# Gates of chunks 1 to 5 computed on 80 partitions, one for each chunk and head, with transfers issued from ScalarE's queue

## The chip, the core and the metric

The kernel runs on one core of one Trainium2 chip. Five engines work beside each other, each through a queue of its own in order: TensorE (PE in the profile, with its weight loads as PEld), VectorE (DVE), ScalarE (ACT), GpSimd (Pool) and SyncE (SP), which here only issues DMAs. The metric is the time of one execution on the device in microseconds; lower is better.

## What is computed

An mLSTM layer over 2 x 8 heads with 768 tokens of 40 channels, then two feed-forward layers on its 1536 tokens of 320 channels. What matters here is the first part, and in it the gates:

```python
for t in range(S):
    m_new = np.maximum(f_gate[:, :, t] + m, i_gate[:, :, t])
    f_stab = np.exp(f_gate[:, :, t] + m - m_new)
    i_stab = np.exp(i_gate[:, :, t] - m_new)
    m = m_new
    C = f_stab * C + i_stab * einsum("bhd,bhe->bhde", vt, kt)
    n = f_stab * n + i_stab * kt
    y[:, :, t] = sigmoid(o_gate) * (C @ qt) / max(|n . qt|, 1)
x = relu_like(y @ w_in) @ w_out              # 320 -> 2048 -> 320
out = sum_e P[:, e] * (relu(x @ w1[e]) @ w2[e])  # 8 experts, 320 -> 1024 -> 320, P by 8 rounds of scaling
```

All products are made in halves of a split (high and low parts in the float32r type), and the result is float32.

## The kernel before

**Tiles and stages.** The 768 tokens are cut into six chunks of 128; a tile is one chunk of one batch entry with its 8 heads, so there are 12 tiles, numbered chunk by chunk. Within a chunk the recurrence becomes matrix products: a scan along the columns makes the 128 x 128 decay matrix of each head (L383, four heads at a time), it is multiplied with the scores (L385), and TensorE multiplies the result with the weighted values (L400). What comes from earlier chunks is the state `Cst` (L395, L407, L412, L440). The result is transposed (L446) and split into `XH` and `XL` (L114, L116).

Four stages of the first feed-forward layer (`STAGES`, `gemm_k` at L124, L541 to L547, `moe1_g2` at L557 to L561) are woven into the tiles; then come the eight experts, which take most of the time (L124 and L704 to L706). The weights of the first layer come as 64-bit floats and are decoded by VectorE and ScalarE (L212 to L256).

**Gates.** Of the gates, two copies of the 16 rows (one for each batch entry and head) lie on 32 partitions, 768 columns each: `g_i`, `g_f` and the running maximum `g_m`, in the tile `g_all`. `gate_exps(a, b)` makes the maximum of columns a to b by a scan (L307), then on the forget gates L310 and L311 and an Exp (L312), on the input gates L313 and an Exp (L314). `gate_prods` makes the running products of the forget gates within each chunk (L326), and writes the forget gates of chunks 1 to 5 to a DRAM buffer `g_d` (L333); `load_g` reads them back for each tile, broadcast to 128 partitions, as the tile `G0` or `G1` (L145). `gate_by_token` transposes gates and products, so that tokens lie on partitions (L340, L341, copied at L342 into `gt`), and `gate_ends` makes the products at the chunks' ends (L346, L353, L354, into `lend`). Chunk 0 has its own short way: its decay comes from products with a one-hot matrix (L376), not from DRAM. The code calls:

```python
gate_exps(0, L); gate_prods(0, 1); gate_by_token(0, 1); gate_exps(L, S)
starts = [attn(0, ("at", "ax")), attn(1, ("g2", "g2"))]
step = 0
while len(done) < 2:
    for g in starts:
        next(g, None)
        warm(WD)
    step += 1
    if step == GP:
        gates_rest()        # gate_prods(1, NCH), gate_by_token(1, NCH), gate_ends(), load_g
    if step in PUMP:
        pump_w()            # one more piece of decoded weights
```

**Order.** The code is written tile by tile; a framework then lists the instructions of each engine in an order of its own by estimated times, keeps the dependencies with semaphores, and each engine works through its list in order. `warm` adds products of a zero tile (L296) of a fixed number. SP issues the DMAs in its list's order; each DMA adds to one of eight semaphores, which are taken in turn, and one that takes a semaphore again waits until the DMA that had it before has landed.

Of the kernel before, what the change touches and what calls it, by code (L numbers as in the profile page):

```python
# [36 lines left out]
GP = 8  # L37
# [11 lines left out]
def mlstm_moe_moe_kernel(  # L49
# [76 lines left out]
    with ExitStack() as atx:  # L126
# [172 lines left out]
        gp.memset(ones, 1.0)  # L299
# [16 lines left out]
        def gate_prods(c0, c1):

            if c0 == 0:
                act(out=g_s, in_=g_f[:, 0:L], func=ACTF.Copy)
                vec.scalar_tensor_tensor(  # L320
                    out=g_s, in0=f(g_s), scalar=cst[0:32, C_N16 : C_N16 + 1], in1=g_f[:, 0:L], op0=ALU.mult, op1=ALU.add,
                )
                vec.tensor_copy(g_s[:, 0:1], zer[:, 0:1])
            for c in range(c0, c1):
                cs = slice(c * L, (c + 1) * L)
                vec.tensor_tensor_scan(out=g_m[:, cs], data0=g_f[:, cs], data1=zer, initial=1.0, op0=ALU.mult, op1=ALU.add)  # L326
            if c0:
                gp.tensor_copy(
                    g_f[:, c0 * L : c1 * L].rearrange("p (c t) -> p c t", t=L)[:, :, 0:1], zer[:, 0 : c1 - c0].unsqueeze(2)
                )  # L330
                for j in range(4):
                    o = j // 2 * 8 + j % 2
                    nc.sync.dma_start(g_d[j * 4 : j * 4 + 4, :], g_f[o : o + 7 : 2, L:S])  # L333

        def gate_by_token(c0, c1):
            p = bank("g1")
            for c in range(c0, c1):
                cs = slice(c * L, (c + 1) * L)
                o = (c - c0) * 32
                nc.tensor.transpose(p[:, o : o + 16], g_i[0:16, cs], ident[0:16, 0:16])  # L340
                nc.tensor.transpose(p[:, o + 16 : o + 32], g_m[0:16, cs], ident[0:16, 0:16])  # L341
# [462 lines left out]
```

## Time and profile before

| | |
|---|---|
| time, median of 3 runs (lowest, highest) | 995.71 us (994.46, 996.32) |
| the profiled execution, its own time | 994.85 us |
| its span, first to last instruction | 993.1 us |
| TensorE busy | 979.6 us, 99% of the span |
| VectorE busy | 470.1 us, 47% |
| ScalarE busy | 344.8 us, 35% |
| GpSimd busy | 31.2 us, 3% |

The span is the time between the first and the last instruction of the profiled execution; its own time has the start and the end around it. Shares are means over stages of different kinds: VectorE has nearly all its work of the first 140 us without a pause, and little later. A row of a timeline says when an instruction, or a row of equal ones, started, how long it was busy, and behind brackets how long its engine had been idle before and what released it.

### The profile page before, as it was taken

The numbers are of one execution on the slowest core, as the hardware profiler recorded it, in microseconds if no ns is written. First come the engines' busy times: TensorE is split into PE (matmuls) and PEld (weight loads), VectorE is DVE, ScalarE is ACT, GpSimd is POOL, SyncE is SP. The second block draws the span as 40 slices with busy tenths as digits, with TensorE's granted clock in tenths as the row PEclk, the third lists the DMA queues.
The fourth block names the chain that finished last, engine by engine and source line by source line (L and its number), as shares of the span: only waits on it lengthen the run. The fifth ranks groups of instructions, "written<-read, shape, count | busy, mean of one in ns | idle before, by whom it ended". The sixth has DMA issues, their size and how long they took to land.

```text
span 993.1 us, 13483 instructions
## 1 busy us (share of the span) xinstructions
PE 979.6 (99%) x5520; PEld 861.8 (87%) x5520; DVE 470.1 (47%) x853; ACT 344.8 (35%) x622; POOL 31.2 (3%) x43
## 2 busy tenths in 40 slices
PE   9999899999999999999999999999999999999998
PEld 5789788887878899999999999989999999999997
DVE  9999977655563644322522432242253234222222
ACT  3743684477773224211411321141132123111111
POOL 2212101000000000000000000000000000000000
PEclk9999999999999999999999999999999999999999
DMA  5865413000132002100400210030021002000000
GB/s 171 263 169 172 143 57 99 12 1 0 47 113 75 1 1 64 54 1 1 117 1 1 74 44 1 7 111 1 1 87 31 1 17 72 1 1 1 27 27 27
DMA packets 42190, 51.91 MB, mean 52 GB/s; under 512 B 3360, under 2 KB 35744, under 8 KB 42128
## 3 DMA queue, kind: packets, MB, share of 16 engines
q1 hardware_dynamic: 42128, 51.05, 17.3%
q8 instruction: 43, 0.70, 0.3%
q14 instruction: 19, 0.16, 0.0%
HBM read 49.03 MB, written 2.01 MB: 51 GB/s over the span
## 4 chain that ended last, share of the span: by engine, by line
PE 89%; DVE 5%; ACT 3%; DMA 1%; issue 1%; SPq 0%; DVEq 0%; ACTq 0%
PE bk_g L124 41%; PE bk_g L704 9%; PE bk_g L706 8%; PE bk_g L705 8%; PE bk_ax L705 3%; PE bk_ax L704 3%; PE bk_ax L706 3%; PE bk_at L400 2%; PE bk_g L296 2%; PE bk_g L559 2%; PE bk_g L558 1%; PE bk_g L557 1%; PE bk_at L379 1%; DMA raw<-in_w_dram 1%; PE bk_g L561 1%
## 5 line engine op out<-in xcount | busy, mean ns | idle before, releaser
L124 PE MATMUL bk_g<-XH,wk 128*128 128x512 f32 (+1 forms) x1240 | 399.8, 388 | 1.6 <-DVE gs L545 1.6
L724 DVE SCALAR_TENSOR_TENSOR lo<-bk_g,hi 128x512 fp32r<-128x512 f32 x192 | 132.6, 691 | 372.6 <-ACT hi L723 371.7
L124 PE MATMUL bk_g<-XL,wk 128*128 128x512 f32 (+1 forms) x744 | 285.4, 384 | 0.0
L723 ACT ACTIVATE hi<-bk_g 128x512 fp32r<-128x512 f32 x192 | 114.9, 599 | 453.2 <-PE bk_g L124 453.0
L124 PEld LDWEIGHTS bk_g<-XH,wk 128*128 128x128 f32 x1240 | 230.6, 188 | 45.1 <-DVE gs L545 2.6
L704 PE MATMUL bk_g<-wf,hi 128*128 128x320 f32 x576 | 177.4, 308 | 1.1 <-ACT hi L723 1.1
L705 PE MATMUL bk_g<-wf,hi 128*128 128x320 f32 x576 | 177.0, 307 | 0.0
L706 PE MATMUL bk_g<-wf,lo 128*128 128x320 f32 x576 | 176.9, 308 | 0.0
L124 PEld LDWEIGHTS bk_g<-XL,wk 128*128 128x128 f32 x744 | 140.0, 188 | 21.4
L704 PEld LDWEIGHTS bk_g<-wf,hi 128*128 128x128 f32 x576 | 108.0, 187 | 8.1 <-ACT hi L723 1.6
L705 PEld LDWEIGHTS bk_g<-wf,hi 128*128 128x128 f32 x576 | 108.1, 188 | 6.3
L706 PEld LDWEIGHTS bk_g<-wf,lo 128*128 128x128 f32 x576 | 107.9, 187 | 0.0
L705 PE MATMUL bk_ax<-wf,hi 128*128 128x320 f32 x192 | 59.1, 308 | 0.0
L704 PE MATMUL bk_ax<-wf,hi 128*128 128x320 f32 x192 | 59.0, 307 | 0.0
L706 PE MATMUL bk_ax<-wf,lo 128*128 128x320 f32 x192 | 58.4, 304 | 0.0
L545 DVE TENSOR_TENSOR gs<-bk_g,gs 128x512 f32<-128x512 f32 x40 | 27.5, 688 | 26.8 <-ACT gs L543 26.4
L541 ACT ACTIVATE gs<-bk_g 128x512 f32<-128x512 f32 x48 | 28.5, 594 | 28.7 <-PE bk_g L124 28.1
L738 DVE SCALAR_TENSOR_TENSOR acc<-bk_g,P,acc 128x320 f32<-128x320 f32 x63 | 30.8, 545 | 15.3 <-PE bk_g L706 15.3
L531 DVE TENSOR_TENSOR wf<-raw,wf 128x640 fp32r<-128x640 f32 x32 | 26.3, 826 | 20.7 <-ACT wf L530 20.5
L704 PEld LDWEIGHTS bk_ax<-wf,hi 128*128 128x128 f32 x192 | 36.1, 188 | 0.0
L706 PEld LDWEIGHTS bk_ax<-wf,lo 128*128 128x128 f32 x192 | 36.1, 188 | 0.0
L705 PEld LDWEIGHTS bk_ax<-wf,hi 128*128 128x128 f32 x192 | 35.9, 187 | 0.0
(198 smaller groups left out, 999.6 us busy)
## 6 DMA issues: line engine op xcount, KB each, us to landing
raw<-in_w_dram SPq DMA_DIRECT2D x32, 320.0 KB
raw<-in_w_dram SPq DMA_DIRECT2D x32, 256.0 KB
kvo_t<-in_kvo_dram SPq DMA_DIRECT2D x12, 484.0 KB
raw<-in_w_out_dram SPq DMA_DIRECT2D x8, 640.0 KB
raw<-in_w_in_dram SPq DMA_DIRECT2D x8, 512.0 KB
raw<-in_w_dram SPq DMA_DIRECT2D x64, 64.0 KB
qk<-in_qk_dram SPq DMA_DIRECT2D x24, 160.0 KB
G<-g_d SPq DMA_DIRECT2D x5, 512.0 KB
```

What stands on the lines that cost most here:

```text
L124: return [mm(dst, a, b, start=i == 0, stop=i == len(seq) - 1) for i, (a, b) in enumerate(seq)]
L296: mm(to, wz, wz[:, 0:1].to_broadcast([128, 512]), start=True, stop=True)
L400: mm(pa[:, h * 41 : (h + 1) * 41], A[h % 2][:, h // 2, :], vw[:, h, :], start=True, stop=True)
L531: vec.tensor_tensor(out=wf[:, fs, 320:640], in0=rs[n], in1=f(wf[:, fs, 0:320]), op=ALU.subtract)
L541: act(out=t, in_=pg, func=ACTF.Relu, scale=-1.0, bias=1.0)
L545: dve_at.append(vec.tensor_tensor(out=g, in0=pg, in1=t, op=ALU.max))
L704: mm(pp[i], hi[:, ts], wf[:, ff, 0:320], start=st, stop=False)
L705: mm(pp[i], hi[:, ts], wf[:, ff, 320:640], start=False, stop=False)
L706: mm(pp[i], lo[:, ts], wf[:, ff, 0:320], start=False, stop=sp)
L723: act(out=hi, in_=pg, func=ACTF.Relu)
L724: vec.scalar_tensor_tensor(out=lo, in0=pg, scalar=0.0, in1=f(hi), op0=ALU.max, op1=ALU.subtract)
L738: vec.scalar_tensor_tensor(out=acc[:, t, :], in0=pp[i], scalar=P[:, t, e : e + 1], in1=acc[:, t, :], op0=ALU.mult, op1=ALU.add)
```

## The change

The gates of chunk 0 are made first (`gates_first`), with their product in a tile of its own, `g_p`. Of chunks 1 to 5 only the scan for the maximum still runs on 640 columns. Then fifteen small transfers, three for each chunk, bring the raw gates (L338 of the new code, from DRAM) and the maximum (L339, from `g_m`) onto 80 partitions, 16 for each chunk, with 128 columns each (`gl_f`, `gl_i`, `gl_m`). All later steps run on these: three element-wise ones and two Exp (L314 to L318), one product scan instead of five (L343), one write of `g_d` with 80 rows (L345), two transposes instead of ten (L347, L348), z and the product for `lend` (L355, L358). The fifteen transfers and the write of `g_d` are issued by ScalarE. The later gates are asked for after step 2 instead of step 8 (`GP`). `load_g` reads each tile's gates in two DMAs of four heads instead of one of eight. The tile `ones` is made at the start of the experts' part instead of at the kernel's start. Ten of the fifteen transfers read from DRAM what SP has also loaded; those of chunks 1 and 2 land where `g_f` lies, so they wait for the long scan.

```diff
@@ load_g
             c, b = divmod(t, 2)
-            nc.sync.dma_start(
-                G1 if t % 2 else G0, g_d[b * 8 : b * 8 + 8, (c - 1) * L : c * L].unsqueeze(0).to_broadcast([128, 8, L])
-            )
+            g, r = G1 if t % 2 else G0, (c - 1) * 16 + b * 8
+            for hf in range(2):
+                nc.sync.dma_start(
+                    g[:, hf * 4 : hf * 4 + 4, :], g_d[r + hf : r + 7 + hf : 2, :].unsqueeze(0).to_broadcast([128, 4, L])
+                )
@@ gates
-GP = 8
+GP = 2
-        gate_exps(0, L)
-        gate_prods(0, 1)
-        gate_by_token(0, 1)
-        gate_exps(L, S)
+        gates_first()
+        def gate_exps(fg, ig, m, m_new):
+            vec.tensor_tensor(out=fg, in0=fg, in1=m, op=ALU.add)
+            vec.tensor_tensor(out=fg, in0=fg, in1=m_new, op=ALU.subtract)
+            act(out=fg, in_=fg, func=ACTF.Exp)
+            vec.tensor_tensor(out=ig, in0=ig, in1=m_new, op=ALU.subtract)
+            act(out=ig, in_=ig, func=ACTF.Exp)
+
+        def gates_first():
+
+            gate_max(0, L)
+            gate_exps(g_f[:, 0:L], g_i[:, 0:L], g_m[:, 0:L], g_m[:, 1 : L + 1])
...
+            gate_max(L, S)
+
+            for c in range(1, NCH):
+                for x, o in ((gl_f, S), (gl_i, 0)):
+                    nc.scalar.dma_start(x[(c - 1) * 16 : c * 16], gates[0:16, o + c * L : o + (c + 1) * L])
+                nc.scalar.dma_start(gl_m[(c - 1) * 16 : c * 16], g_m[0:16, c * L : (c + 1) * L + 1])
+
+        def gates_later():
+            gate_exps(gl_f, gl_i, gl_m[:, 0:L], gl_m[:, 1 : L + 1])
+            vec.tensor_tensor_scan(out=gl_p, data0=gl_f, data1=cst[0:NLR, C_Z : C_Z + 1].to_broadcast([NLR, L]), initial=1.0, op0=ALU.mult, op1=ALU.add)
+            gp.tensor_copy(gl_f[:, 0:1], cst[0:NLR, C_Z : C_Z + 1])
+            nc.scalar.dma_start(g_d, gl_f)
+            p = bank("g1")
+            nc.tensor.transpose(p[:, 0:NLR], gl_i, ident[0:NLR, 0:NLR])
+            nc.tensor.transpose(p[:, NLR : 2 * NLR], gl_p, ident[0:NLR, 0:NLR])
...
@@ experts
+        ones = m2.tile([128, 128], F32, name="ones")
+        gp.memset(ones, 1.0)
```

What it does to the lists is seen at three places. In the rows, names are those of the tiles, with buffer numbers; in brackets stand the semaphores that an instruction waits for: those of an engine's progress (`DVE_49`, `PE_49`, `Activation_49`, `Pool_49`) and the eight of the DMAs (`DMAHW0_49` to `DMAHW7_49`). Line numbers of the changed kernel are higher by 3 to 5 for the same code.

VectorE, from the long scan of the maximum on, before:

```order
L307 SCALAR_TENSOR_TENSOR g_all_80<-g_all_80 32x640
L310 TENSOR_TENSOR g_all_80<-g_all_80 32x640 [waits DVE_49]
L326 SCALAR_TENSOR_TENSOR g_all_80<-g_all_80,cst_64 32x128 [waits DMAHW2_49,Activation_49]
L320 SCALAR_TENSOR_TENSOR g_s_110<-g_s_110,cst_64,g_all_80 32x128 [waits Activation_49]
L311 TENSOR_TENSOR g_all_80<-g_all_80 32x640 [waits DVE_49]
L323 CAST g_s_110<-cst_64 32x1 [waits DVE_49]
L313 TENSOR_TENSOR g_all_80<-g_all_80 32x640
L326 SCALAR_TENSOR_TENSOR g_all_80<-g_all_80,cst_64 32x128 [waits DVE_49,Activation_49]
L326 SCALAR_TENSOR_TENSOR g_all_80<-g_all_80,cst_64 32x128 x2
L383 SCALAR_TENSOR_TENSOR G0_90<-bk_at_166,id4_116 128x512 [waits PE_49,Pool_49]
L326 SCALAR_TENSOR_TENSOR g_all_80<-g_all_80,cst_64 32x128
L385 TENSOR_TENSOR A_207<-bk_at_171,G0_90 128x512 [waits DVE_49,PE_49]
```

The same place in the changed kernel:

```order
L309 SCALAR_TENSOR_TENSOR g_all_79<-g_all_79 32x640
L329 SCALAR_TENSOR_TENSOR g_p_111<-g_all_79,cst_64 16x128 [waits DMAHW7_49,Activation_49]
L325 SCALAR_TENSOR_TENSOR g_s_110<-g_s_110,cst_64,g_all_79 32x128 [waits Activation_49]
L328 CAST g_s_110<-cst_64 32x1 [waits DVE_49]
L388 SCALAR_TENSOR_TENSOR G0_90<-bk_at_176,id4_117 128x512 [waits PE_49,Pool_49]
L390 TENSOR_TENSOR A_234<-bk_at_181,G0_90 128x512 [waits DVE_49,PE_49]
L388 SCALAR_TENSOR_TENSOR scr_87<-bk_g2_190,id4_117 128x512 [waits PE_49]
L314 TENSOR_TENSOR g_all_79<-g_all_79,gl_m_86 80x128 [waits DMAHW5_49,DMAHW6_49,DMAHW4_49,DMAHW7_49,DMAHW3_49,DMAHW0_49]
L317 TENSOR_TENSOR g_all_79<-g_all_79,gl_m_86 80x128 [waits DMAHW2_49,DMAHW1_49]
L315 TENSOR_TENSOR g_all_79<-g_all_79,gl_m_86 80x128 [waits DVE_49]
L390 TENSOR_TENSOR scr_87<-bk_g2_195,scr_87 128x512 [waits PE_49]
L388 SCALAR_TENSOR_TENSOR G0_90<-bk_at_247,id4_117 128x512 [waits PE_49]
```

The rows of chunks 1 to 5 have gone from between the steps of tiles 0 and 1 (L383 and L385 before, L388 and L390 now); in their place stand L314, L317 and L315 on 80 partitions, the first with waits for six of the eight DMA semaphores.

ScalarE, from the copy of chunk 0's gates by token on, before:

```order
L342 ACTIVATE gt_113<-bk_g1_144 128x32 [waits PE_49]
L312 ACTIVATE g_all_80<-g_all_80 32x640 [waits DVE_49]
L314 ACTIVATE g_all_80<-g_all_80 32x640 [waits DVE_49]
L402 ACT_TABLE_LOAD
L402 ACTIVATE sg_291<-kvo_t_102 128x320 [waits DMAHW5_49]
L402 ACTIVATE sg_307<-kvo_t_106 128x320 [waits DMAHW0_49]
L212 ACTIVATE dv_201<-raw_194 128x512 [waits DMAHW1_49]
L212 ACTIVATE dv_250<-raw_196 128x512 [waits DMAHW2_49]
```

The same place in the changed kernel:

```order
L333 ACTIVATE gt_114<-bk_g1_144 128x32 [waits PE_49]
L338 DMA g_all_79<-in_gates_dram 16x128 [waits DMAHW5_49]
L339 DMA gl_m_86<-g_all_79 16x129
L338 DMA g_all_79<-in_gates_dram 16x128 [waits DMAHW0_49]
L338 DMA g_all_79<-in_gates_dram 16x128 [waits DMAHW1_49]
L339 DMA gl_m_86<-g_all_79 16x129 [waits DMAHW3_49]
L339 DMA gl_m_86<-g_all_79 16x129 [waits DMAHW4_49]
L339 DMA gl_m_86<-g_all_79 16x129 [waits DMAHW5_49]
L339 DMA gl_m_86<-g_all_79 16x129 [waits DMAHW7_49]
L407 ACT_TABLE_LOAD
L407 ACTIVATE sg_318<-kvo_t_102 128x320
L318 ACT_TABLE_LOAD [waits DMAHW2_49,DMAHW1_49]
```

Behind that copy now stand eight DMA issues, of which seven wait for an earlier DMA's landing, then a table load for the Sigmoid of tile 0 and a table load back for the Exp.

TensorE, ahead of the last scores of tile 1, in the changed kernel (before, the row of four warm-up products is not broken up, and the gates' transposes come after tile 1's attention):

```order
L300 LDWEIGHTS wz_91
L300 MATMUL bk_g2_93<-wz_91 128x512
L347 MATMUL bk_g1_212<-cst_64,g_all_79 128x80 [waits DMAHW1_49,DMAHW5_49,DMAHW0_49,Activation_49]
L300 LDWEIGHTS wz_91
L300 MATMUL bk_g2_93<-wz_91 128x512
L300 LDWEIGHTS wz_91
L300 MATMUL bk_g2_93<-wz_91 128x512
L381 MATMUL bk_g2_261<-g_s_110,m16_r_112 128x128 [waits DVE_49]
L348 MATMUL bk_g1_212<-cst_64,g_all_79 128x80 [waits DVE_49]
L381 MATMUL bk_g2_261<-g_s_110,m16_r_112 128x128
L358 MATMUL bk_g1_218<-z_216,cst_64 104x40 [waits DVE_49]
L381 MATMUL bk_g2_261<-g_s_110,m16_r_112 128x128 x2
```

The two transposes (L347, L348) and the product of the chunk ends (L358) have moved in between the warm-up products (L300) and the products that make chunk 0's decay (L381).

## Rows read from the trace of the kernel before

**Rows 1.** Busy time of each engine (instructions) by stretch, granted clock, DMA share.

```profile
core 0: us, PE busy (x) PEld busy (x) DVE busy (x) ACT busy (x) POOL busy (x), PEclk, DMA share, GB/s
...
8.24:27.70 19.46, 19.46 (x127) 13.97 (x128) 19.21 (x35) 7.63 (x12) 3.50 (x5) 1.00 0.62 171
...
20.00:140.00 120.00, 113.88 (x801) 97.64 (x799) 114.38 (x223) 70.34 (x141) 20.48 (x21) 0.99 0.54 160
```

**Rows 2.** TensorE's timeline: start, us, engine, line, operation, out<-in, count.

```profile
10.00 0.66 PE L376 MATMUL bk_at<-g_s,m_r 32*128 32x128 f32 x4
10.59 1.16 PE L379 MATMUL bk_at<-qk 104*128 104x128 f32 x8
...
12.27 1.48 PE L296 MATMUL bk_g<-wz 128*128 128x512 bf16 x6
...
18.03 1.16 PE L379 MATMUL bk_g<-qk 104*128 104x128 f32 x8
19.03 2.78 PE L296 MATMUL bk_g<-wz 128*128 128x512 bf16 x12
...
31.80 0.23 PE L340 MATMUL bk_g<-cst,g_all 16*128 16x16 f32 x1
...
32.44 0.36 PE L353 MATMUL bk_g<-z,cst 16*104 16x48 f32 x2
```

**Rows 3.** VectorE's timeline, the gate rows.

```profile
5.14 0.28 DVE L310 TENSOR_TENSOR g_all<-g_all 32x128 f32<-32x128 f32 x1
...
5.75 1.53 DVE L307 TENSOR_TENSOR_SCAN g_all<-g_all 32x640 f32<-32x640 f32 x1
7.32 0.81 DVE L310 TENSOR_TENSOR g_all<-g_all 32x640 f32<-32x640 f32 x1
...
9.44 1.28 DVE L313 TENSOR_TENSOR g_all<-g_all 32x640 f32<-32x640 f32 x1
10.82 1.04 DVE L326 TENSOR_TENSOR_SCAN g_all<-g_all,cst 32x128 f32<-32x128 f32 x3
...
13.81 0.40 DVE L326 TENSOR_TENSOR_SCAN g_all<-g_all,cst 32x128 f32<-32x128 f32 x1
...
15.25 0.17 DVE L346 TENSOR_TENSOR z<-g_all,cst 16x48 f32<-16x48 f32 x1
```

**Rows 4.** VectorE's timeline, first and last decoding step before tile 1's last product.

```profile
17.96 0.45 DVE L213 TENSOR_SCALAR dv<-dv 128x512 f32<-128x512 f32 x1
...
21.99 0.41 DVE L214 TENSOR_SCALAR dv<-dv 128x512 int32<-128x512 int32 x1
22.32 0.68 DVE L385 TENSOR_TENSOR scr<-bk_g,scr 128x512 f32<-128x512 f32 x1
```

**Rows 5.** ScalarE's timeline, with idle time before and what ended it.

```profile
4.19 0.21 ACT L303 ACTIVATE m_r<-cst 32x16 fp32r<-32x16 f32 x1 [2.17 <-DMA cst<-in_consts_dram]
5.86 0.31 ACT L312 ACTIVATE g_all<-g_all 32x128 f32<-32x128 f32 x1 [1.45 <-DVE g_all L311]
...
8.92 0.20 ACT L342 ACTIVATE gt<-bk_g 128x32 f32<-128x32 f32 x1 [2.35 <-PE bk_g L341]
...
11.51 1.28 ACT L402 ACT_TABLE_LOAD   x1
```

**Rows 6.** SP's DMA issues, and the Pool step released by the last.

```profile
0.74 0.39 SPq L137 DMA_DIRECT2D g_all<-in_gates_dram  x1
...
1.64 0.42 SPq L139 DMA_DIRECT2D cst<-in_consts_dram  x1
...
14.54 0.65 SPq L333 DMA_DIRECT2D g_d<-g_all  x1
...
32.66 0.42 SPq L163 DMA_DIRECT2D kvo_t<-in_kvo_dram  x1
...
38.64 3.73 POOL L365 TENSOR_TENSOR vw<-kvo_t,gt 128x328 f32<-128x328 f32 x1 [17.46 <-DMA kvo_t<-in_kvo_dram]
```

**Rows 7.** TensorE's waits, whole run: total us, times, longest.

```profile
PE bk_g L557 <- ACT XH L546: 2.1, 2, 1.9
```

More of the change, by code (lines that the diff above doesn't have):

```diff
@@ L135, in mlstm_moe_moe_kernel @@
         dram = ctx.enter_context(tc.tile_pool(name="dram", bufs=1, space=bass.MemoryType.DRAM))
-        g_d = dram.tile([16, S - L], F32, name="g_d")
+        NLR = (NCH - 1) * 16
+        g_d = dram.tile([NLR, L], F32, name="g_d")
         nc.sync.dma_start(g_f, gates[:, S : 2 * S])
@@ L139, in mlstm_moe_moe_kernel @@
         nc.sync.dma_start(cst, consts)
+        gl_i, gl_f, gl_p = (g_all[0:NLR, 1024 + i * L : 1024 + (i + 1) * L] for i in range(3))
+        gl_m = ap.tile([NLR, L + 1], F32, name="gl_m")
         gates_done = []
@@ L283, in mlstm_moe_moe_kernel @@
         zer = cst[0:32, 32 : 32 + L]
+        g_p = ap.tile([16, L], F32, name="g_p")
         m16_r = ap.tile([32, 16], F32R, name="m16_r")
@@ L298, in mlstm_moe_moe_kernel @@
         warm(W0)
-        gp.memset(ones, 1.0)
         for kw in kws:
@@ L316, in gate_prods @@
[L316 to L333, printed above, removed]
@@ L335, in gate_by_token @@
-        def gate_by_token(c0, c1):
-            p = bank("g1")
[L337 to L341, printed above, removed]
-            act(out=gt[:, c0:c1, :], in_=p[:, 0 : 32 * (c1 - c0)].rearrange("p (c e) -> p c e", e=32), func=ACTF.Copy)
-        def gate_ends():
-            z = ap.tile([16, NCH, 8], F32, name="z")
-            vec.tensor_tensor(
-                out=z,
-                in0=g_m[0:16, 0:S].rearrange("p (c t) -> p c t", t=L)[:, :, L - 1 : L].to_broadcast([16, NCH, 8]),
-                in1=cst[0:16, C_PM : C_PM + 8].unsqueeze(1).to_broadcast([16, NCH, 8]),
-                op=ALU.mult,
+        def gate_exps(fg, ig, m, m_new):
[4 more added lines that the diff above has]
+            act(out=ig, in_=ig, func=ACTF.Exp)
@@ new lines, in gates_later @@
+        def gates_later():
[6 more added lines that the diff above has]
+            nc.tensor.transpose(p[:, NLR : 2 * NLR], gl_p, ident[0:NLR, 0:NLR])
+            act(
+                out=gt[:, 1:NCH, :].rearrange("p c (w r) -> p w c r", w=2),
+                in_=p[:, 0 : 2 * NLR].rearrange("p (w c r) -> p w c r", w=2, r=16), func=ACTF.Copy,
+            )
+            z = ap.tile([NLR, (NCH - 1) * 8], F32, name="z")
+            vec.tensor_scalar(
+                out=z, in0=cst[0:NLR, C_PM : C_PM + (NCH - 1) * 8], scalar1=gl_p[:, L - 1 : L], scalar2=None, op0=ALU.mult,
@@ L351, in gate_ends @@
             )
             p = bank("g1")
-            mm(p[0:104, 0 : NCH * 8], cst[0:16, C_W : C_W + 104], z.rearrange("p c e -> p (c e)"), start=True, stop=True)
-            act(out=lend, in_=p[0:104, 0 : NCH * 8], func=ACTF.Copy)
+            mm(p[0:104, 0 : (NCH - 1) * 8], cst[0:NLR, C_W : C_W + 104], z, start=True, stop=True)
+            act(out=lend[:, 8 : NCH * 8], in_=p[0:104, 0 : (NCH - 1) * 8], func=ACTF.Copy)
         def attn(t, tags):
@@ L755, in _consts @@
         c[r, C_M16 + r % 16] = 1.0
-    for r in range(16):
-        c[r, C_PM + r // 2] = 1.0
+    for r in range((NCH - 1) * 16):
+        c[r, C_PM + r // 16 * 8 + r % 16 // 2] = 1.0
         c[r, C_W + (r % 2) * 64 : C_W + 64 + (r % 2) * 40] = 1.0
```

29 lines of the change are left out of this document (15 added, 14 removed).

## The prediction, made before the changed kernel ran

> **What bounds the kernel now.** I read the engine table by stretch first. Over the whole run TensorE (PE) hardly stops; in the first 140 us VectorE (DVE) is nearly as full: 114.38 of 120 us between 20 and 140 [rows 1]. A gain has to come out of that part, since the change touches nothing later except where the tile `ones` lives. So the question is which of the two engines sets the pace where the gates are made, 4.6 to 23 us. The second view is PE's timeline there. Its stream is fixed: warm-up products (L296) and the attention products of tiles 0 and 1. It is not waiting: from 8.24 to 27.70 it is busy for all 19.46 us [rows 1], and its starts follow one another at the pace of the products themselves, four L376 in 0.59 us, the instructions of four L379 in 1.16 us (1.1 to the next start), a warm-up in 0.22 to 0.25 us [rows 2]. The third view is DVE's timeline: it has no gap either, and the gate work of chunks 1 to 5 lies between its attention steps, from 5.75 to 15.4 us [rows 3]. Two engines, both full, one of them with a stream that the change does not shorten: that is the point on which the forecast turns.
>
> **DVE's gate work.** Before, chunks 1 to 5 cost on 640 columns one scan for the maximum (1.53 us), L310 and L311, of one form (0.81 each), L313 (1.28), five product scans (some 0.39 each) and L346 (0.17) [rows 3]. The first scan stays. The rest, 0.81 + 0.81 + 1.28 + 1.97 + 0.17 = 5.04 us, becomes three operations on 128 columns (0.28 by the row of that width [rows 3]), one product scan (0.39) and a small product for z (0.17): 1.40 us. On 80 partitions instead of 32 I take the same time for the same columns; the trace has attention steps on 128 partitions and nothing that would make partitions dear. DVE saves 3.6 us of work.
>
> **What that is worth.** I walk both queues with the durations of before. In the new order PE does three warm-ups fewer ahead of the first L381 (0.7 us), so that product starts at 9.3 instead of 10.00 [rows 2] and ends at 9.9; the four L384 end at 11.0, the next four L381 at 11.6; nine warm-ups bring 13.7, then L381 13.9, L384 15.0, three L381 15.45, L384 16.55, two warm-ups 17.0. DVE ends the long scan at 7.28, the product scan of chunk 0 at 7.7, two short steps of chunk 0 by about 8.1, and has nothing to do until 9.9, since the rows that filled this time are gone. Its first scan runs 9.9 to 11.1, the product 11.1 to 11.7, the scan of tile 1 to 12.85. Then comes L314, the first step of the later gates. It takes 0.65 us with L317 and L315, and the step after it (L390) cannot start before PE's 15.0. So 14.35 is the latest harmless start. From there PE leads again: L390 to 15.65, scan to 16.8, product to 17.45, then product scan L343 to 17.85 and z to 18.0. PE now has the two transposes and the product of the gates inside this stretch (L347, L348, L358, 0.2 us each by L340's row of 0.21 to L353's 0.36 for two [rows 2]); it reaches the end of its last L384 at 19.5, against 19.03 before [rows 2]. DVE finishes the last product of tile 1 at 20.3. Before, it had finished that product and six steps of the weights' decoding (17.96 to 22.32 less the attention scan, 3.2 us together) at 22.9 [rows 4]: 19.7 without them. So DVE is not 3.6 us ahead but **0.6 us behind**. The saved work turns into waits for PE's fixed stream. From there DVE has the same steps to do as before, almost without gaps, so 0.6 us goes through to the end. The ten transposes and the product that PE loses at 31.80 to 32.7 [rows 2] give 0.9 us back to PE alone, which waits for DVE and ScalarE (ACT) soon after.
>
> **The small transfers.** L314 waits for fifteen transfers, and whatever DVE has to do next, the attention of both tiles, is queued behind it. Six are issued before ACT's first table load, 9 later. ACT copies the by-token gates at 8.92 before [rows 5], 0.2 us earlier now, then issues eight in a row. One issue costs SP 0.39 us (gates, 32 rows) to 0.65 (g_d, 4 rows) [rows 6]; with the former, rounded to 0.4, the eighth goes out at 8.9 + 7 * 0.4 = 11.7. It must also wait for the landing of the second of the eight, whose semaphore it takes over. Time to landing: 2.55 us for `cst` in a nearly empty machine (issued 1.64, ACT released at 4.19), 6.0 us for 484 KB among other loads (32.66 to 38.64) [rows 5, 6]. These are 8 KB pieces, so I take the near end, 2.55: the second, out at 9.3, lands at 11.85, the eighth lands at 14.4. That is DVE's 14.35: cost 0.05 us. The ends: 0 with free issues, and 7 us with 6.0 twice (9.3 + 12.0 = 21.3). A gain below nothing is excluded, as a wait cannot end before its transfers start.
>
> The Trainium skill (DMA: Bandwidth & Descriptors, Rules for kernel authors) says to coalesce small transfers, as one under 64 KB is mostly overhead; its anatomy section puts the fixed part at about 2.0 us. By that estimate the eighth would land at 13.7 and the wait would be nil; the sum hardly moves.
>
> **ACT.** The two Exp on 640 columns become two on 128, of 0.3 us [rows 5]. The functions now alternate, Exp, Sigmoid, Exp, Sigmoid, so there are two more table loads of 1.28 us [rows 5]. The last issue ends at 12.25; load 13.5, Sigmoid 14.0, load 15.3, Exp of the input gate 15.6, of the other 15.8. Needed: 17.0 (PE's L347) and 17.45 (DVE's L343). Hidden with 1.4 us to spare; without that cover, 2.6 us. Then the second Sigmoid, the write of g_d (behind Pool's copy at 17.9 and so at 18) and the two copies end near 19, in time for the decoding at 20.3. The first six issues (2.3 us and a landing) and the load end near 4.6; the Exp of chunk 0 starts at 5.9, so they cost nothing.
>
> **SP.** It loses four writes of g_d (0.65 us the first [rows 6]) and gets ten more loads of G, of half the size, spread over 100 us in which it waits for buffers: nothing; without that cover ten issues of 0.4. The first weight load now waits for a gate transfer's semaphore, to about 12 us; its decoding starts at 19, and 512 KB at the stretch's 171 GB/s [rows 1] take 3.1 us, so nothing. The memset of `ones` moves to Pool's idle time: nothing.
>
> **Sum.** Against the profiled execution (994.85 us, 0.86 below the median of the three runs, within their spread): +0.6 + 0.05. On the median, 995.71 + 0.6 = **996.3 us**, which is no change: 0.2% is 2.0 us, about the least that a measurement of this kernel can tell.
>
> **Rivals.**
> 1. *The saving arrives.* If PE had waited in 8 to 20 us without the profile showing it, DVE's 3.6 us less 0.3 of new waits would go through: 992.4. For it: both engines look equally full, and a modelled end of a product can hide a wait. Against: starts at full pace in every piece of the stretch. Chance 0.14.
> 2. *A later wait goes.* PE waits 2.1 us for XH (L557 for L546) in one piece of 60 to 70 us [rows 7], and its idle time from 20 to 140 us is 120 - 113.88 = 6.1 us in all [rows 1]. The list of instructions there comes out differently; if that takes this wait and a third of the rest, 2.1 + 1.4 = 3.5 us: 992.2. Against: DVE's steps before it are the same ones in the same number. Chance 0.14.
> 3. *The transfers come late, slower.* L314 holds DVE, and through L348 PE. It decides from a landing at 15.8 on (0.6 + 1.4 us late). With 3.7 us to landing, a third of the way to the far end: 9.3 + 3.7 = 13.0, landing 16.7, 2.35 late, with the 0.6: 998.7; at the far end 1003. For it: eight issues in a row and weight loads in flight on the same DMA engines. Chance 0.17.
> 4. *Table loads dearer than their rows.* If a load between the two sets took twice its row (2.6 us), the Exps would end at 18.4 and hold PE and DVE for 1.4 us: 995.7 + 2.1 = 997.8. Against: both loads of before take 1.28 us. Chance 0.04. The Trainium skill speaks against this change here (ScalarE: Activation LUTs, Rules for kernel authors): group activations by table set, and count some 2.7 us for each switch. By that figure this rival would be the forecast; the trace has less than half of it.
> 5. *The new order falls worse* elsewhere by 2 us or more: 998.5, chance 0.05.
>
> **How the numbers follow.** The forecast has 0.46, the faster cases 0.28, the slower ones 0.26. Faster by over 0.2%: 0.28; within: 0.46; slower: 0.26. The range runs from 992.2 (rivals 1 and 2 at their full price) to 999.2 (rival 3 at the latency taken). The far end of the landing time is left out.
>
> **What the new profile would show.** DVE idle for some 1.8 us from 8.1 us on, released by PE's L381; L314 at 12.9 to 14.4 after a wait for the transfers; ACT's last issue near 12; PE's twelve warm-ups starting at 19.5 +- 0.4; decoding from 20.3. The forecast is wrong if PE's row at that place stands before 18 (rival 1), if L314 starts after 15.8 (rival 3), or if the XH wait near 64 us is gone (rival 2).

## The result: 10.9 us slower, and the profile after

The changed kernel takes 1006.3 us (median of 6, 1004.6 to 1009.8), the kernel before 995.4: a ratio of 1.0114, 95% interval 1.0093 to 1.0134. The forecast was no change, 996.3. The profiled execution took 1009.8 us, its span 1008.0 against 993.1.

First TensorE's timeline in the changed kernel (start, us, engine, line, operation, out<-in, count, idle time before and its releaser). L381, L384 and L300 are L376, L379 and L296 of before.

```profile
15.67 0.60 PE L300 MATMUL bk_g<-wz 128*128 128x512 bf16 x2
19.21 0.40 PE L347 MATMUL bk_g<-cst,g_all 80*128 80x80 f32 x1 [2.94 <-ACT g_all L318]
...
21.96 0.40 PE L348 MATMUL bk_g<-cst,g_all 80*128 80x80 f32 x1 [1.10 <-DVE g_all L343]
...
23.80 2.08 PE L384 MATMUL bk_g<-qk 104*128 104x128 f32 x8
25.67 3.96 PE L300 MATMUL bk_g<-wz 128*128 128x512 bf16 x12
```

The same eight products and twelve warm-ups stood at 18.03 and 19.03 before, with 1.16 and 2.78 us [rows 2]. They come 5.8 and 6.6 us later, and they take longer: there is idle time now, and the clock is lower behind it. VectorE's timeline shows who holds them:

```profile
11.24 1.21 DVE L388 TENSOR_TENSOR_SCAN scr<-bk_g,id 128x512 f32<-128x512 f32 x1
18.32 0.29 DVE L314 TENSOR_TENSOR g_all<-g_all,gl_m 80x128 f32<-80x128 f32 x1 [5.87 <-DMA gl_m<-g_all]
...
23.91 1.23 DVE L388 TENSOR_TENSOR_SCAN scr<-bk_g,id 128x512 f32<-128x512 f32 x1 [1.72 <-PE bk_g L381]
25.91 0.69 DVE L390 TENSOR_TENSOR scr<-bk_g,scr 128x512 f32<-128x512 f32 x1 [0.78 <-PE bk_g L384]
26.52 0.75 DVE L216 TENSOR_SCALAR dv<-dv 128x512 f32<-128x512 f32 x2
```

L314, forecast for 12.9 to 14.4, starts at 18.32, and decoding (L216) at 26.5 in place of 20.3. The gate steps themselves are as short as forecast (0.29 us; [rows 3] have 0.81 to 1.28). The table by stretch (busy us of each engine with its instructions, granted clock, DMA share, GB/s) answers [rows 1]:

```profile
8.24:27.70 19.46, 15.42 (x72) 10.01 (x71) 9.79 (x17) 6.92 (x11) 3.13 (x5) 0.75 0.70 175
16.00:28.00 12.00, 7.96 (x26) 4.73 (x25) 7.04 (x15) 3.88 (x8) 1.66 (x3) 0.58 0.67 148
54.00:60.00 6.00, 5.13 (x25) 3.70 (x25) 5.09 (x9) 3.60 (x6) 0.74 (x1) 0.72 0.60 176
78.00:84.00 6.00, 5.73 (x34) 5.21 (x33) 5.91 (x13) 2.02 (x4) 0.80 (x1) 0.72 0.61 194
174.00:182.00 8.00, 7.86 (x37) 7.33 (x37) 5.54 (x12) 0.00 (x0) 1.68 (x2) 0.57 0.55 166
20.00:140.00 120.00, 109.70 (x761) 92.99 (x760) 107.70 (x213) 62.23 (x126) 21.67 (x23) 0.94 0.56 165
```

Where the two engines were full before (19.46 and 19.21 us of 19.46), TensorE now has 15.42 and VectorE 9.79. Four stretches have a granted clock well below 1, that is TensorE at its level of 1.2 GHz for most of them. The kernel before has one such stretch, 66 to 72 us.

TensorE's wait of [rows 7], for XH, isn't gone but has more than doubled:

```profile
PE bk_g L559 <- ACT XH L548: 5.1, 2, 3.5
```

To see where the time is lost I follow one step through the kernels: L116 (XL, the last step of a tile's attention on VectorE), by its start in each profiled execution. "Half clock" lists the stretches, in steps of 2 us, whose granted clock is under 0.97 (0.50, that is 1.2 GHz, inside). The ratio is that of the means, against executions of the kernel before taken beside each kernel (their medians go from 995.4 to 996.5 us), so it isn't the quotient of two medians of the table. Of *again*'s six executions one, at a mean clock of 0.85, took 1079.8 us; it and one such of the kernel before are left out. The positions come from one execution of each kernel.

| kernel | median, ratio to before (95%) | span | L314 | L116: tile 0 | tile 2 | tile 7 | tile 8 | half clock (us) |
|---|---|---|---|---|---|---|---|---|
| before | 995.4 | 993.1 | - | 36.3 | 55.4 | 113.1 | 169.9 | 66-72 |
| changed | 1006.3, 1.0114 (1.0093-1.0134) | 1008.0 | 18.3 | 45.9 | 66.9 | 124.1 | 184.1 | 16-28, 54-60, 78-84, 174-182 |
| again | 1009.1, 1.0103 (1.0068-1.0138) | 998.4 | 14.4 | 38.9 | 58.7 | 116.5 | 174.6 | 70-74 |
| own5 | 1007.9, 1.0126 (1.0103-1.0150) | 1010.6 | 19.9 | 49.5 | 71.7 | 128.9 | 187.3 | 16-34, 58-66, 180-186 |
| hold | 1006.0, 1.0107 (1.0086-1.0128) | 1002.1 | 14.8 | 39.9 | 60.9 | 118.1 | 177.9 | 48-54, 168-176 |
| warm | 1005.2, 1.0094 (1.0067-1.0122) | 1001.5 | 14.5 | 39.6 | 59.3 | 117.1 | 178.1 | 70-76, 166-178 |
| pe_m | 1004.4, 1.0080 (1.0061-1.0099) | 1001.4 | 12.8 | 38.5 | 59.5 | 117.2 | 177.5 | 48-52, 168-176 |
| pe_pin | 1002.5, 1.0056 (1.0036-1.0077) | 1000.2 | 12.9 | 38.4 | 58.0 | 115.7 | 177.1 | 68-74, 164-176 |
| pin_wd3 | 999.2, 1.0034 (1.0009-1.0058) | 996.2 | 12.4 | 36.9 | 56.9 | 114.2 | 174.0 | 44-50, 164-174 |
| shift8 | 998.4, 1.0025 (1.0010-1.0040) | 996.9 | - | 36.2 | 55.3 | 112.9 | 174.1 | 66-72, 164-174 |
| shift20 | 1000.0, 1.0044 (1.0030-1.0059) | 998.2 | - | 36.8 | 56.4 | 114.1 | 175.3 | 68-72 |
| b_wd2 | 1007.5, 1.0106 (1.0059-1.0153) | 1007.4 | - | 40.9 | 65.2 | 124.7 | 184.1 | 14-32, 38-50, 72-84, 174-182 |

In the profiled execution of the changed kernel 9.5 us are lost by the first L116, 1.9 by tile 2's, nothing to tile 7's, 3.2 by tile 8's. Three causes were open: the late landing, the half clock, the new list of instructions.

### The profile page after: what moved, and what is told of

Same layout as the page of the kernel before. It is cut to its first block, busy times and chain, and to the rows that moved or that the text cites. A ratio compares the mean times of both kernels' runs of the same rounds, so it can differ in the third digit from the quotient of the medians.

```text
span 1008.0 us, 13504 instructions
## 1 busy us (share of the span) xinstructions
PE 986.9 (98%) x5512; PEld 867.8 (86%) x5512; DVE 467.3 (46%) x849; ACT 345.4 (34%) x624; POOL 31.6 (3%) x43
## 4 chain that ended last, share of the span: by engine, by line
PE 87%; DVE 6%; ACT 3%; DMA 3%; issue 1%; SPq 0%; ACTq 0%; DVEq 0%
PE bk_g L124 40%; PE bk_g L708 8%; PE bk_g L710 8%; PE bk_g L709 8%; PE bk_ax L708 3%; PE bk_ax L709 3%; PE bk_ax L710 3%; PE bk_at L405 2%; PE bk_at L384 1%; PE bk_g L561 1%; PE bk_g L560 1%; PE bk_g L559 1%; PE bk_g L300 1%; DMA raw<-in_w_dram 1%; PE bk_g L563 1%
## 5 line engine op out<-in xcount | busy, mean ns | idle before, releaser
L708 PE MATMUL bk_g<-wf,hi 128*128 128x320 f32 x576 | 177.9, 309 | 1.5 <-ACT hi L727 1.5
L708 PE MATMUL bk_ax<-wf,hi 128*128 128x320 f32 x192 | 59.5, 310 | 0.0
```

Of the source, the lines that this page charges most:

```text
L708: mm(pp[i], hi[:, ts], wf[:, ff, 0:320], start=st, stop=False)
```

## Experiments on the landing

**The changed kernel again** (no edit).

> The changed kernel once more, unchanged. Landing theory: its times scatter over 5 us (1004.6 to 1009.8) because the last transfer of m lands anywhere between 14.5 and 18.3 us, so the profiled execution of this run may show L314 between 14.4 and 18.5, and its span follows: near 1003 with L314 at 14.5 (as the kernel with more warm-ups had by its own trace), near 1008 with 18.3. If the landing is always late: L314 at 18 and a span of 1003 or 1008 alike.

Its profiled execution took 1000.16 us, span 998.4, four others 1007.1 to 1009.6. In that one execution VectorE, SP and ScalarE show:

```profile
14.40 0.29 DVE L314 TENSOR_TENSOR g_all<-g_all,gl_m 80x128 f32<-80x128 f32 x1 [1.45 <-DMA gl_m<-g_all]
...
19.29 1.22 DVE L388 TENSOR_TENSOR_SCAN scr<-bk_g,id 128x512 f32<-128x512 f32 x1 [1.02 <-PE bk_g L381]
...
21.22 0.79 DVE L216 TENSOR_SCALAR dv<-dv 128x512 f32<-128x512 f32 x2
```
```profile
12.84 0.98 SPq L198 DMA_DIRECT2D raw<-in_w_in_dram  x2
```
```profile
10.49 2.44 ACTq L339 DMA_DIRECT2D gl_m<-g_all  x4
```

and in the first profiled execution of the changed kernel SP and ScalarE had

```profile
11.26 0.83 SPq L198 DMA_DIRECT2D raw<-in_w_in_dram  x2
```
```profile
9.98 2.43 ACTq L339 DMA_DIRECT2D gl_m<-g_all  x4
```

One issue of m takes 0.60 us, so the last starts at 10.49 + 2.44 - 0.60 = 12.33 here and at 11.81 there. Here the weight loads (512 KB each) are issued after it, and L314 starts 2.1 us behind it; there they were issued 0.55 us ahead of it, and L314 starts 6.5 us behind it. SP's weight load waits for the semaphore of a gate transfer, so which comes first is a race that a microsecond decides.

**Own room, fewer transfers** (own5). f and i of a chunk in one early transfer, in a decoding buffer:

```
+        gl = dec.tile([128, 640], F32, name="dv", tag="dv", bufs=2)
+        gl_i, gl_f, gl_p = (gl[0:NLR, i * L : (i + 1) * L] for i in range(3))
...
+                nc.scalar.dma_start(
+                    gl[(c - 1) * 16 : c * 16, 0 : 2 * L].rearrange("p (x t) -> p x t", x=2),
...
```

> The changed kernel, but the later gates have room of their own (a buffer of the weights' decoding), so that f and i of a chunk come in one transfer, five in all, that are issued at the start; after the long scan only the five transfers of m are issued. Landing theory (the 11 us come from the step L314, which stood 5.87 us for the last transfer of m, issued at 11.81 and landed at 18.2 behind weight loads): the last of m goes out by 10.9, ahead of the weight loads at 11.3, and lands by 14.5; the wait before L314 is under 2 us, TensorE isn't idle at 16 to 19 and keeps a granted clock of 1.00 there; time 995 to 999. Order theory (the new list of instructions is worse by itself, wherever L314 starts): 1002 or more.

L314's step (L315 there) starts at 19.92: worse, against my expectation.

```profile
19.92 0.29 DVE L315 TENSOR_TENSOR dv<-dv,gl_m 80x128 f32<-80x128 f32 x1 [6.32 <-DMA gl_m<-g_all]
```
```profile
10.21 0.82 SPq L199 DMA_DIRECT2D raw<-in_w_in_dram  x2
```
```profile
9.04 2.47 ACTq L342 DMA_DIRECT2D gl_m<-g_all  x4
```

The last m goes out at 10.9 as expected, but the weight loads had been freed earlier too, to 10.21, and are ahead of it again: 9.0 us from issue to L314's step.

**Weight loads held** (hold).

```
+            if hold:
+                hold.pop()
+                gp.tensor_copy(r[0:NLR, 0:1].bitcast(F32), gl_m[:, 0:1])
```

> The changed kernel, but the first three weight loads wait until the transfers of m have landed (a one-column copy of m into their buffers, which the loads overwrite, stands ahead of them). Landing theory with the weight loads as the cause of the late landing: the last m, issued near 11.8, lands by 14.5 to 15, as the first gate transfers did (2 to 3 us after their issue); L314 at 14.5 to 15.5, weights 4 us later, still ahead of their decoding at 20.5; time 996 to 1000. If the landing is late for a reason of its own (the queue of ScalarE, many small pieces): L314 at 18 as before, weights at 22, time 1007 to 1010. Order theory: over 1002 in both cases.

```profile
14.79 0.29 DVE L319 TENSOR_TENSOR g_all<-g_all,gl_m 80x128 f32<-80x128 f32 x1 [1.85 <-DMA gl_m<-g_all]
```
```profile
15.15 0.81 SPq L203 DMA_DIRECT2D raw<-in_w_in_dram  x2
```
```profile
10.47 2.43 ACTq L344 DMA_DIRECT2D gl_m<-g_all  x4
```

The loads go out at 15.15, the last m at 12.30, L314's step (L319 there) starts at 14.79: the landing is as expected. The time isn't: 1006.0, as the order theory had it (over 1002). With *warm* (weight loads at 13.47, last m at 12.51, L314 at 14.52) that makes five traces: weight loads ahead of the last m, 6.5 and 9.0 us to L314; behind it, 2.0 to 2.5. In all five the order of issue goes with the time, and *hold* changed that order: the collision is shown. Yet without it the median hardly moves (1006.0 against 1006.3).

**m by products, no transfer after the scan** (pe_m): f and i as in *own5*, m by TensorE.

```
+            gl_m = bank("g1")[0:NLR, 0 : L + 1]
+            for c in range(1, NCH):
+                e = C_ID - (c - 1) * 16
+                mm(gl_m, cst[0:16, e : e + NLR], g_m[0:16, c * L : (c + 1) * L + 1], start=c == 1, stop=c == NCH - 1)
```

> As the kernel with room of its own for the later gates, but m comes to the 80 partitions by five small products of TensorE with a shifted identity, in place of five transfers: no step of VectorE waits for a transfer that starts after the long scan. Landing theory: L314 at 12.5 to 13.5, TensorE without idle time at 16 to 19, clock 1.00; time 994 to 997, the five products costing TensorE 1 to 1.5 us. Order theory: 1002 or more, since the new list is kept. The rival that VectorE's saving would arrive once the wait is gone: 991 to 993.

L314 at 12.8, TensorE without idle time there, clock 1.00 to 48 us, and still 1004.4: the landing theory as the whole cause falls. The products that bring m take 1.3 us of TensorE. VectorE's waits from 8 to 38 us (total, times, longest), and its row by stretch, from the end of the long scan to the end of tile 1's L116, then that of the kernel before between the same two steps:

```profile
DVE G L393 <- PE bk_at L386: 2.2, 2, 1.3
DVE scr L395 <- PE bk_g L389: 1.3, 1, 1.3
DVE dv L248 <- ACT wk L246: 1.0, 1, 1.0
```
```profile
7.50:39.60 32.10, 31.29 (x199) 21.46 (x200) 27.09 (x56) 18.17 (x36) 4.16 (x6) 1.00 0.75 215
```
```profile
7.28:37.36 30.08, 29.86 (x189) 19.62 (x188) 29.69 (x60) 16.09 (x33) 3.50 (x5) 1.00 0.66 187
```

VectorE works 2.6 us less for the same steps of attention and decoding, and stands 5.0 us in place of 0.4. The saving does turn into waits, 3.5 of them for TensorE's row of products, and L248's is new: L246 is queued on ScalarE behind copies of the state (L447), which wait for TensorE.

**Warm-ups in TensorE's gap** (warm), ahead of L347:

```
+WL = 12
...
             nc.scalar.dma_start(g_d, gl_f)
+            warm(WL)
```

> The changed kernel with twelve more warm-up products ahead of the two transposes L347, L348, where TensorE stood 2.9 us for L318; nothing else is changed. L314 stays at 18 to 18.5. Clock theory (part of the loss is TensorE at half clock from 16.3 to 28, eight L384 taking 2.08 us in place of 1.16 and twelve warm-ups 3.96 in place of 2.78): clock 1.00 at 20 to 28, decoding at 25 in place of 26.5, time 1003 to 1005. If the clock costs nothing because VectorE's wait alone sets the end: 1006 to 1007.

It became no test of the clock: its L314 came at 14.5, and the gap wasn't there. It serves as a trace of the landing.

## Experiments on the clock

Between the L116 of tiles 7 and 8 the kernels with half clock there lose 1.6 to 4.6 us against *before* (shifts taken off), those without 0 to 1.5. The products there are the same, and TensorE's wait is nearly so. *before*, *changed*, *shift8*, *shift20*, in this order:

```profile
161.97 0.39 PE L400 MATMUL bk_at<-vw,A 128*128 128x41 f32 x2 [1.10 <-DVE A L385]
...
163.27 1.75 PE L400 MATMUL bk_at<-vw,A 128*128 128x41 f32 x14
164.86 0.94 PE L407 MATMUL bk_at<-vw,kw 128*104 128x82 f32 x8
```
```profile
172.94 0.39 PE L405 MATMUL bk_at<-vw,A 128*128 128x41 f32 x2 [1.12 <-DVE A L390]
...
174.24 2.68 PE L405 MATMUL bk_at<-vw,A 128*128 128x41 f32 x14
176.72 1.66 PE L412 MATMUL bk_at<-vw,kw 128*104 128x82 f32 x8
```
```profile
163.50 0.39 PE L400 MATMUL bk_at<-vw,A 128*128 128x41 f32 x2 [1.07 <-DVE A L385]
...
164.81 2.32 PE L400 MATMUL bk_at<-vw,A 128*128 128x41 f32 x14
166.92 1.66 PE L407 MATMUL bk_at<-vw,kw 128*104 128x82 f32 x8
```
```profile
167.31 0.39 PE L400 MATMUL bk_at<-vw,A 128*128 128x41 f32 x2 [1.08 <-DVE A L385]
168.61 1.76 PE L400 MATMUL bk_at<-vw,A 128*128 128x41 f32 x14
170.19 0.94 PE L407 MATMUL bk_at<-vw,kw 128*104 128x82 f32 x8
```

**The kernel before, only shifted** (shift8, shift20; n = 8, 20), with instructions otherwise in the same order:

```
+                        if si == 1 and hf == 1 and ff == 9:
+                            warm(n, pg)
```

> The kernel before with nothing changed but eight warm-up products more on TensorE in the stage of the 512-column products, some 20 us ahead of tile 8: the same list of instructions, shifted by 8 * 0.22 = 1.8 us. Order theory (the loss near 170 us comes with the new list): the granted clock stays 1.00 from 155 to 185, time 995.9 + 1.8 = 997.2 to 997.8. Clock theory (the loss near 170 us is TensorE's clock falling after the wait of 1.1 us for tile 8's L385, which both lists have; whether it falls depends on when in the run the wait comes): a fall to 0.50 behind that wait is possible at this shift, time then 1000 to 1001.

> As the one with eight, with twenty warm-up products, a shift of 4.4 us, which brings the wait of tile 8 to the time at which the kernel with m by products has it (165 to 166 us). Order theory: 995.9 + 4.4 = 1000 to 1000.5, clock 1.00. Clock theory: a fall to 0.50 from about 168 to 176 as in that kernel, 3 us more, 1003 to 1003.6.

In *shift8*'s profiled execution the fall is there: tile 8's L116 comes 4.1 us late in place of 1.8; the median, 998.4, lies between the two numbers expected. *shift20*'s has no fall, 1000.0, the bare shift. So the fall near 170 us needs neither the change nor its list. That the shift of 1.8 us brings it isn't shown: there is one trace of each kernel, and the executions of *shift8* have mean clocks of 0.994 and 0.995 (three) and 0.997 and 0.998 (three). The kernel before, unshifted, has such slower executions too: of 57, 45 at 0.998 or more take 994.4 to 997.5 us, four at 0.995 take 997.9 to 999.2, three at 0.993 take 1000.7 to 1001.8. My reading that a shift to 165 us must bring the fall was wrong: *pe_m* falls there and *shift20* doesn't. What decides it stays open.

The Trainium skill (TensorE: Matmul & The Clock Gate, the part on the clock gate) calls the gate's watch free-running, not started by the kernel, so that a change of clock depends on where the work falls in it. The executions of one kernel, with and without a lower clock, agree with that; no run here shows the watch itself.

**Shifts of the family, and a filled wait.** pe_sh12 is *pe_m* with 12 of these products, pin_sh8 and pin_sh20 are *pe_pin* (below) with 8 and 20. pe_t8 is *pe_m* with

```
-            if 2 <= t < 8:
+            if 2 <= t < 9:
                 warm(WA, pa)
```

> The kernel with m by products of TensorE, shifted by twelve warm-up products (2.6 us) at the place of the shifts of the kernel before; the list is otherwise the same. If the fall of the clock behind tile 8's wait is a matter of when it comes (clock theory), it may be missed here: then L116 of tile 8 stands 2.6 - 3.5 = 0.9 us earlier than without the shift, time 1003.5; with the fall kept, time 1007.

> The pinned kernel with m by products, shifted by eight warm-up products (1.8 us) ahead of tile 8; the list is otherwise the same. Clock theory: if the fall behind tile 8's wait is missed at this shift, time 1002.5 + 1.8 - 3.5 = 1000.8 or a little less; with it, 1004.3.

> As the one with eight, with twenty (4.4 us), the shift at which the kernel before had no fall. Missed fall: 1002.5 + 4.4 - 3.5 = 1003.4; with it: 1006.9.

> The kernel with m by products of TensorE, and in addition four warm-up products ahead of tile 8's L410, as tiles 2 to 7 have them: they fill 0.9 of the 1.4 us that TensorE waits there. Clock theory: no fall to half clock at 168 to 176, which took 3 to 3.5 us; time 1001 to 1001.5, less the 0.4 in which the products may run over the wait. Order theory: 1004 to 1005, since the order stays.

pe_sh12 keeps the fall (168 to 176 in its profiled execution) with 1005.0, between the two numbers; of its six executions one, 1001.9, has a mean clock of 0.998, the others 0.992 to 0.995. pin_sh8 keeps it (170 to 178), 1002.4, also between. pin_sh20's profiled execution, 1009.7, has no fall there, but half clock from 12 to 30; its four others take 1003.7 to 1004.2 where 1003.4 was expected without the fall. pe_t8, 1004.3, told nothing: the four products stood behind the same wait (L300 for L395, 1.3 us), so nothing was filled.

**The list at tile 8.** The traces without a fall there are of two kinds: *shift20*, in the old list, loses nothing between the two L116; *again*, pe_wd2 and pin_sh20, in the new one, lose 1.3 to 1.5 us. *before*, then *again*, VectorE and TensorE:

```profile
166.71 0.31 DVE L440 TENSOR_TENSOR Cst<-bk_at,Cst 40x164 f32<-40x164 f32 x1
...
170.40 1.21 DVE L383 TENSOR_TENSOR_SCAN G<-G,id 128x512 f32<-128x512 f32 x1
```
```profile
167.63 0.46 PE L379 MATMUL bk_at<-qk 104*128 104x128 f32 x2 [0.21 <-DVE Cst L440]
```
```profile
168.86 1.22 DVE L388 TENSOR_TENSOR_SCAN G<-G,id 128x512 f32<-128x512 f32 x1
...
171.57 0.31 DVE L445 TENSOR_TENSOR Cst<-bk_at,Cst 40x164 f32<-40x164 f32 x1
```
```profile
172.50 0.68 PE L384 MATMUL bk_at<-qk 104*128 104x128 f32 x4 [1.23 <-DVE Cst L445]
```

A scan of 1.2 us that stood behind tile 8's L116 now stands ahead of its state step, and TensorE waits 1.2 us for the state (1.2 and 1.6 in the two others) in place of 0.2. This part of the loss is the list's, without any half clock. Why the list came out so was not tested; all kernels with the change keep `load_g` in two halves, which may have moved the scan.

## Experiments on the list and the fixed stream

**Later gates asked for as before** (pe_gp8), *pe_m* with

```
-GP = 2
+GP = 8
```

> The kernel with m by products of TensorE, but the later gates are asked for after step 8 as before the change, in place of step 2: their steps on VectorE then stand behind the attention of tiles 0 and 1 and behind decoding. Order theory (0.6 to 1 us of waits for TensorE's fixed stream at 9 to 18 us and 1 us of a wait behind the copies of the state on ScalarE come with the early place): the first L116 stands within 1 us of the kernel before or ahead of it, time 999 to 1002, the rest being the clock near 170 us. If the early place is not what costs: 1004 to 1005 as with it.

The first L116 comes at 31.8, 4.5 us ahead of the kernel before, but the later gates' last step ends at 41 us, and tile 2's L116 comes at 63.6, 8.2 behind: 1008.0, ratio 1.0119 (1.0104 to 1.0134). Asking late gains on tile 0 and loses more by tile 2, so the early place by itself isn't what costs.

**Two places put back** (pe_pin):

```
+                with tc.issue_after(dve_at[0].ins) if len(dve_at) == 1 else ExitStack():
                     vec.tensor_tensor(out=wk[:, 2 + k, cs], in0=w, in1=f(wk[:, k, cs]), op=ALU.subtract)
...
+                        with tc.issue_after(r_at[0].ins):
                             act(out=Cst[rs, b, :, es], in_=puv[rs, :, es], func=ACTF.Copy)
```

> The kernel with m by products of TensorE, with two places of the list put back to the order before the change: ScalarE's L246 ahead of the copies of the state (L248 on VectorE waited 1.0 us behind them), and the weight step L239 behind the first L554's maximum on VectorE, as it stood before (0.6 us). Order theory: the first L116 1 us earlier than without (37.5), the third by 1.5 us, time 1002.5 to 1003. If these places don't matter: 1004 to 1005.

The median is as the order theory expected, 1002.5; the steps only in part. L248's wait is gone, but one of 1.1 us for L215 takes its place and the first L116 moves by 0.2, not 1. Tile 2's comes 1.5 us earlier, as expected; but *pe_m* had half clock just there (48 to 52) and *pe_pin* had not, so list and clock aren't told apart.

**Fewer warm-ups** (pe_wd2: *pe_m* with `WD = 2` in place of 4; b_wd2: the kernel before with the same; pin_wd3: *pe_pin* with `WD = 3`). Two are 36 products fewer in all, three 18; the 16 to 18 of the first expectation were miscounted.

> The kernel with m by products of TensorE, with two warm-up products after each step of the attention of tiles 0 and 1 in place of four, some 16 to 18 fewer in all (3.5 to 4 us of TensorE). Theory of the fixed stream (VectorE's saving turns into waits for TensorE's row of products, 3.5 us of such waits at 9 to 18 us in the kernel with four): the waits shrink to under 1.5 us and the first L116 comes 2 us or more earlier than with four, at or ahead of the kernel before (36.3); time 1001 to 1002.5, unless TensorE's clock falls in the idle time that opens. If the stream isn't what holds VectorE: L116 stays at 38.5, time 1004 to 1005.

> The kernel before with two warm-up products in place of four, the control: VectorE had no wait there (29.05 of 29.40 us busy from 8 to 37.4), so by the theory of the fixed stream the shorter stream brings nothing here: the first L116 within 0.5 us of 36.3, time 995 to 997. If it gains 2 us or more, the stream held the kernel before too, and the prediction's reading of two equally full engines was wrong.

> The pinned kernel with three warm-up products in place of four after each step of tiles 0 and 1 (1.8 to 2 us less of TensorE). Theory of the fixed stream: VectorE's waits of 4.6 us shrink by 1 to 2 us, and the first L116 comes as much earlier (near 37), 1000.5 to 1001.5. If TensorE falls to half clock in the idle time that opens, as with two: L116 at 40 or later in the profiled execution, time over 1002.

pin_wd3 is better than expected: waits for TensorE of 1.7 us in place of 3.5 (the one for L215 grows to 1.9), first L116 at 36.9, 999.2 us, the nearest that any kernel with the change came to the one before; it too has the fall at 164 to 174. Its one execution of ten at a mean clock of 0.998 took 996.1 us, as the kernel before. pe_wd2's median is 1001.4, ratio 1.0054 (1.0035 to 1.0074), as expected; the steps of its profiled execution are not (first L116 at 42.2 in place of 36.3 or earlier; span 1002.7): it has half clock at 16 to 24, 36 to 42, 50 to 56 and 74 to 80. The control is the surprise. VectorE had no wait to lose there, and the kernel before became 1.06% slower, 1007.5 us. Its rows by stretch:

```profile
14.00:32.00 18.00, 17.78 (x82) 16.04 (x84) 9.90 (x20) 1.98 (x5) 2.35 (x4) 0.53 0.25 56
38.00:50.00 12.00, 7.14 (x33) 5.68 (x34) 11.87 (x26) 7.22 (x15) 1.29 (x1) 0.57 0.71 212
```

Half clock for most of 30 us goes with a loss as large as that of the whole change under study. The warm-ups that VectorE now waits for also keep the clock up: with a part of them gone it fell there.

## Why the prediction was wrong

- **VectorE's saving turns into waits: right.** The walk through both queues holds to within 0.9 us where the transfers land in time: in *again* L314 starts at 14.40 (forecast 14.35 to 14.4), the last eight L384 end near 20.2 (forecast 19.5) and decoding starts at 21.2 (forecast 20.3; 0.9 late, since L381 waits behind L348, which waits 0.5 us for L343). That L314 is met so closely is luck: the last issue starts 0.5 us later than forecast (12.33, not 11.85), and lands 0.5 us sooner after it (2.07, not 2.55).
- **"0.6 us goes through to the end": the step that failed.** It says that from 20.3 us on VectorE has the same steps as before, almost without gaps, and it prices them all at full clock. *again*, with the landing in time and a mean clock of 0.998 as before, ends 5.3 us behind: 2.6 by the first L116, 0.7 by tile 2's, 1.3 by tile 8's, the rest later. The steps are the same, but their places in the lists aren't: L248 waits 1.6 us for L246, and a scan ahead of tile 8's state step holds TensorE for 1.2. Neither was a term of the sum. Rival 5 had this with 0.05.

```profile
31.78 0.68 DVE L248 TENSOR_TENSOR dv<-raw,wk 64x512 fp32r<-64x512 f32 x1 [1.58 <-ACT wk L246]
```

- **TensorE's clock: put at nothing without a reason.** Every duration came from rows at full clock. In the profiled execution the gap of 2.94 us is followed by half clock to 28 us, and the first L116 is 7.0 us later than in *again*, landing and clock together. Eleven executions of the changed kernel line up by their mean clock: 1000.2 us at 0.998, 1004.6 at 0.993 and 0.995, 1006.1 to 1007.1 at 0.991 and 0.992, 1008.4 to 1009.6 at 0.990, 1009.8 at 0.988; at the same mean clock of 0.993 to 0.998 they are 3.5 to 6 us behind the kernel before.
- **Landing in 2.55 us, "SP ... nothing": wrong too, but not what the median hangs on.** It is 2.0 to 2.5 us with the weight loads behind, 6.5 and 9.0 with them ahead. I had the weight loads freed by a gate transfer's semaphore near 12 us and didn't set that time beside the last m's 11.7. Rival 3 named the collision but gave it 0.17, and its price left out what follows. With the landing put right the kernels still take 1006.0 (*hold*) and 1004.4 (*pe_m*). The Trainium skill (DMA: Bandwidth & Descriptors, the anatomy of one DMA) gives about 2.0 us fixed for a transfer, fitted on those that GpSimd issues; the three transfers ahead of the loads, issued by ScalarE, are near it, the two behind them aren't.
- **ScalarE's own work: right.** Its last issue ends at 12.4 (forecast 12.25), and the table loads take 1.28 us as before. The Trainium skill (ScalarE: Activation LUTs, Rules for kernel authors) counts some 2.7 us for each switch; here 1.3 us lie between the end of the step ahead of a load and the start of the one behind it (16.54 to 17.85 in *again*).
- **Rival 2** (a later wait goes) went the other way: 5.1 us in place of 2.1, and 4.9 in *again*, so it comes without a late landing; *again* loses only 0.1 us from tile 2's L116 to tile 7's.
- **Two sums** of the prediction don't come out: a third of the rest of TensorE's idle time (6.1 - 2.1 us) is 1.3, not 1.4, and rival 3's working gives 998.7, not the range's 999.2. Neither bears on the result.

Settled: the collision and what it costs L314, the saving lost in waits, 1.2 us of the list at tile 8, and that a fall of the clock near 170 us needs neither the change nor its list. Of the median's 10.9 us some 5 are there without late landing and with no more half clock than before (*again*, one execution). The rest goes with the clock; that the clock makes it is argued from the line of executions above, since no run holds the clock, and that late landing adds to the median isn't shown. Not settled: what lets the clock fall in one execution and not in another, and how much of the 5 us beyond L248's wait and tile 8 is the list. No run puts back the halves of `load_g` or the issuing by SP alone. No kernel here beats the one before.

## What to carry to other kernels

Work taken off an engine that runs beside a fixed stream was worth nothing here until the stream was shortened too, and a stream that holds the clock can't be shortened freely: price the idle time that a change opens on TensorE with durations at half clock. Compare the two lists beyond the stage that the change touches: a step may have moved there. Before moving small transfers onto the critical path, list by time what large loads the same semaphores set free, and keep those behind them. Compare several executions by their mean clock, and the kernel before among them, before a difference is put down to the change; a shift by a few warm-ups, the list unchanged, shows whether a loss needs the change at all.

## What the runs showed of the hardware that I had not expected

- An 8 KB transfer issued 0.55 to 0.7 us behind the first 512 KB load let its reader start 6.5 and 9.0 us after its issue; issued ahead of it, 2.0 to 2.5 us.
- The same products behind the same wait of 1.1 us ran at half clock in one profiled execution and not in others: fourteen 128x41 products took 2.32 us (*shift8*) or 1.75 and 1.76 (*before*, *shift20*).
- The kernel before, one program, took 994.4 to 997.5 us at a mean clock of 0.998 or more and 1000.7 to 1001.8 at 0.993.
- Thirty-six warm-up products fewer, some 8 us of TensorE's work, made the kernel before 1.06% slower, with a granted clock of 0.53 from 14 to 32 us and 0.57 from 38 to 50.
